# The early rows of the first expert get tiles of their own and are loaded inside the attention pipeline

## The chip, the core and the metric

One core of a Trainium2 chip runs the kernel. The metric is the device time of one execution in microseconds (us), the median of three runs. The engines have a program each and meet through semaphores: TensorE (PE, matmuls and transposes), VectorE (DVE), ScalarE (ACT), GpSimd (POOL), and SyncE (SP), which only issues transfers (DMA). An engine takes its instructions strictly in the order of its program.

## The reference

Chunked local attention is followed by a mixture of experts. The shapes are 4 batches, 8 heads, 768 positions, 64 per head; queries go in chunks of 32 that see 16 positions to the left, 8 to the right and 8 memory positions.

```python
scores = scale * np.matmul(q_c, k_full.transpose(0, 1, 3, 2))
scores = scores - np.max(scores, axis=-1, keepdims=True)
a = np.exp(scores)
a = a / (np.sum(a, axis=-1, keepdims=True) + 1e-09)
out[:, :, c_start:c_end] = np.matmul(a, v_full)
```

The result is read as 3072 tokens of 512 numbers. Each token goes to the one of 8 experts whose logit is largest, at most 768 tokens to an expert, first come first served, and the result is weighted with the softmax probability.

```python
logits = x @ w_gate
expert_idx = np.argmax(logits, axis=1)
...
h = np.maximum(np.einsum('ecd,edf->ecf', disp, w1), 0.0)
y = np.einsum('ecf,efd->ecd', h, w2)
```

All is fp32. Each expert matmul is done as three: both operands are split into a high part and the remainder (`hi` and `lo`), and hi·hi, lo·hi and hi·lo are added.

## The kernel before, in words

**Attention** runs over 24 tiles of 128 tokens, steps t = 0 to 23. In one step PE does the scores of tile t (L508), transposes of keys or queries for later tiles (trans_k L474, trans_q L462), the transposes of the exponentials of tile t-1 (`trans_p`, L532), the product with the values of tile t-2 (`value`, L549), the transposes of the attention output of tile t-3 (`trans_out`, L602), and, once per group of tiles, the routing logits (L626, for the last group L617). DVE takes the row maximum m (L516) and the difference d (L519), scales the output (rc L552 and L554, xr L557) and copies overlapping value rows into the next value tile vw (L413, L414). SP loads values and weights in program order. What is left after step 23 is called the drain: trans_p(23), value(22), value(23) and what follows them.

**Routing** is done for seven groups of tiles, (first tile, number): (0,4), (4,4), (8,4), (12,4), (16,3), (19,3), (22,2), numbered 0 to 6. `route(g)` is a chain of short DVE rows with PE work in between: r_m, r_d, r_t, r_idx, r_oh (the one-hot choice, L660), then PE counts the tokens ahead (L665 to L669), then r_sel, r_cnt, `seen` (the running count per expert, L680), r_den, r_pos, r_ov, r_slot, r_dst. It is a Python generator, and `tick` lets it go on by one row, so the places of the ticks set where these rows stand in each engine's program. When r_dst is there, POOL puts the group's token rows into the DRAM buffer x_d by indirect transfers, one per tile (`put`, L796): each row goes to its slot with its expert. After the last group the finish chain (L709 to L741) works out the counts, the slots to be filled with padding (`pads`) and flags for the branches.

**Early rows** are the first 256 rows (two tiles) of expert 0. They are complete once group 3 has been routed if at least 256 tokens have chosen expert 0 by then; the flag `ok` says so. `early_rows` loads them into xg (L309) after the last value product; `early` transposes them (L322), multiplies them with w1 of expert 0 (layer 1, L331 and L340) and applies relu (L341, L342), in pieces that the ticks of groups 5 and 6 are interleaved with. Each of the eight pieces f holds 12 matmuls. w2 is split into w2hi and w2lo (`split2`, ACT L847 and DVE L848). Their layer 2 (L911) stands at the start of `expert(0)`.

**Experts.** For each expert: load its rows (`load_x`, L818), transpose them (`trans_x`, L832, with xhi on ACT L836 and xlo on DVE L837), layer 1 (L856), relu (L869, L870), layer 2 (L911), scaling (y, L917) and an indirect store of the tokens (L918). For expert 0 the transposes stand between pieces of the second half of the early layer 2. `values` loads flags into registers of the engines. `fill(e)` writes padding rows to the unused slots of expert e (POOL).

## Time and profile before

| what | value |
|---|---|
| median of 3 runs (lowest, highest) | 512.57 us (512.25, 512.99) |
| profiled execution, its own time | 512.2 us |
| span of its instructions | 510.3 us |
| mean granted PE clock | 0.974 of full |
| busy: PE, DVE, ACT, POOL | 464.8, 303.3, 240.0, 117.0 us |
| start of scores(20), (21), (22), (23) | 119.13, 124.63, 130.36, 135.57 us |
| early rows: load issued, first transpose | 149.56, 153.55 us |
| early layer 2, first and expert 0's layer 1, first | 170.48, 183.61 us |

The page gives each engine's busy time, the waits and the chain of work that ended last; timelines list single rows with their start, duration and the idle time ahead of them with what ended it. Idle time of PE can be read in brackets; the granted clock is read from rows by windows of time. DMA rows show when a transfer was issued and the chain how long it took to land.

### The profile page before, as it was taken

Reading aid. Unit: us, or ns where it says so; the run is one execution under the profiler, and the core shown is the slowest. Engines: PE = TensorE matmul, PEld = TensorE weight load, DVE = VectorE, ACT = ScalarE, POOL = GpSimd, SP = SyncE. Lnnn points to the kernel's source line nnn. Section 1 sums busy time; section 2 is a strip of 40 time slices with the busy share of each in tenths; the row PEclk is TensorE's granted clock in tenths of the full one; section 3 lists DMA queues with packets and bytes.
Section 4 is the critical chain, followed back from the end, with each engine's and each line's share of the span. In section 5 each row is a group of like instructions: output and inputs, shape, how many; then the busy total and the mean of one; then the engine's idle time right before and its main releaser. Section 6 shows DMA issues by size and latency. Waiting matters only on the chain.

```text
span 510.3 us, 11844 instructions
## 1 busy us (share of the span) xinstructions
PE 464.8 (91%) x4321; PEld 397.0 (78%) x4321; DVE 303.3 (59%) x673; ACT 240.0 (47%) x462; POOL 117.0 (23%) x151
## 2 busy tenths in 40 slices
PE   7789997998859898998999999999999799699993
PEld 6677876776649788886778899799888788687882
DVE  5989797999945742565644535655434365655410
ACT  6698787788622432534444234434412353453300
POOL 7531134554624370110200200100021002010011
PEclk9999999999987998999999999999999799999998
DMA  9687879974672484355363281461413343640010
GB/s 208 141 211 178 201 238 268 214 194 109 150 261 96 163 316 143 134 185 181 123 226 116 100 296 33 170 207 56 166 62 111 134 166 104 211 182 9 3 41 38
DMA packets 77775, 78.44 MB, mean 154 GB/s; under 512 B 31762, under 2 KB 58510, under 8 KB 77648
## 3 DMA queue, kind: packets, MB, share of 16 engines
q1 hardware_dynamic: 72848, 61.93, 41.8%
q0 software_dynamic: 4800, 14.95, 7.6%
q8 instruction: 64, 1.05, 0.8%
q14 instruction: 63, 0.52, 0.3%
HBM read 60.86 MB, written 15.99 MB: 151 GB/s over the span
## 4 chain that ended last, share of the span: by engine, by line
DMA 39%; issue 32%; PE 13%; DVE 7%; ACT 2%; POOL 2%; SPq 2%; POOLq 1%; DVEq 0%; ACTq 0%
DMA out_dram<-y,tok 30%; DMA x_d<-pad,pads 4%; PE ps L549 3%; PE ps L508 2%; PE ps L462 2%; DMA x_d<-xr,r_dst 2%; ACT kw L479 2%; DVE vw L414 1%; PE ps L602 1%; PE ps L331 1%; PE ps L474 1%; DMA vw<-in_v_dram 1%; DMA memv<-in_mem_v_dram 1%; PE ps L532 1%; POOL vw L135 1%
## 5 line engine op out<-in xcount | busy, mean ns | idle before, releaser
L869 ACT ACTIVATE hhi<-p 128x512 fp32r<-128x512 f32 x68 | 40.7, 598 | 146.5 <-PE p L856 116.7
L918 POOL DMA_INDIRECT out_dram<-y,tok x28 | 31.8, 1134 | 282.7 <-DVEq L840 148.8
L870 DVE SCALAR_TENSOR_TENSOR hlo<-p,hhi 128x512 fp32r<-128x512 f32 x68 | 47.0, 691 | 77.2 <-ACT hhi L869 72.8
L911 PE MATMUL p<-w2hi,hhi 128*128 128x512 f32 x224 | 91.6, 409 | 1.3 <-DVE hlo L342 1.3
L911 PE MATMUL p<-w2lo,hhi 128*128 128x512 f32 x224 | 88.0, 393 | 0.0
L911 PE MATMUL p<-w2hi,hlo 128*128 128x512 f32 x224 | 87.6, 391 | 0.0
L856 PE MATMUL p<-xhi,w1hi 128*128 128x320 f32 (+3 forms) x288 | 61.0, 334 | 9.4 <-DVEq L900 5.6
L856 PE MATMUL p<-xhi,w1lo 128*128 128x320 f32 (+3 forms) x288 | 59.1, 328 | 0.0
L856 PE MATMUL p<-xlo,w1hi 128*128 128x320 f32 (+3 forms) x288 | 58.7, 326 | 0.0
L856 PEld LDWEIGHTS p<-xhi,w1hi 128*128 128x128 f32 x288 | 47.0, 195 | 13.1 <-issue 5.2
L917 DVE TENSOR_SCALAR y<-p,xg 128x512 f32<-128x512 f32 x28 | 21.0, 749 | 53.7 <-PE p L911 32.2
L911 PEld LDWEIGHTS p<-w2hi,hlo 128*128 128x128 f32 x224 | 42.1, 188 | 9.9
L856 PEld LDWEIGHTS p<-xhi,w1lo 128*128 128x128 f32 x288 | 47.4, 194 | 2.8
L911 PEld LDWEIGHTS p<-w2hi,hhi 128*128 128x128 f32 x224 | 42.2, 188 | 9.4 <-ACT w2hi L847 1.4
L856 PEld LDWEIGHTS p<-xlo,w1hi 128*128 128x128 f32 x288 | 47.0, 192 | 2.8
L911 PEld LDWEIGHTS p<-w2lo,hhi 128*128 128x128 f32 x224 | 42.2, 188 | 7.6
L837 DVE TENSOR_TENSOR xlo<-px,xhi 128x512 fp32r<-128x512 f32 x34 | 23.3, 690 | 32.0 <-ACT xhi L836 32.0
L479 ACT COPY kw<-ps 64x256 f32<-64x256 f32 x92 | 35.5, 386 | 11.8 <-PE ps L474 10.5
L848 DVE TENSOR_TENSOR w2lo<-raw,w2hi 128x512 fp32r<-128x512 f32 x64 | 41.0, 682 | 0.0
L836 ACT CAST xhi<-px 128x512 fp32r<-128x512 f32 x34 | 19.8, 588 | 43.8 <-PE px L832 36.3
L822 DVE TENSOR_TENSOR w1lo<-raw,w1hi 128x512 fp32r<-128x512 f32 x56 | 36.6, 685 | 2.9 <-ACT w1hi L821 1.0
L847 ACT CAST w2hi<-raw 128x512 fp32r<-128x512 f32 x64 | 36.1, 618 | 0.0
(154 smaller groups left out, 707.8 us busy)
## 6 DMA issues: line engine op xcount, KB each, us to landing
raw<-in_moe_w_dram SPq DMA_DIRECT2D x16, 2048.0 KB
raw<-in_q_dram SPq DMA_DIRECT2D x11, 512.0 KB
raw<-in_k_dram SPq DMA_DIRECT2D x10, 512.0 KB
vw<-in_v_dram SPq DMA_DIRECT2D x57, 64.0 KB
xg<-x_d SPq DMA_DIRECT2D x3, 792.0 KB
vw<-in_v_dram SPq DMA_DIRECT2D x31, 72.0 KB
xg<-x_d SPq DMA_DIRECT2D x4, 528.0 KB
xg<-x_d SPq DMA_DIRECT2D x2, 1056.0 KB
```

What stands on the lines that cost most here:

```text
L479: (nc.vector.tensor_copy if n == 0 and i else nc.scalar.copy)(out=kw[r, 2 * i:2 * i + 2, :, hf, 24 + j:56:2], in_=ps[j * 64:j * 64 + 64, h ...
L822: (eng or self.nc.vector).tensor_tensor(out=lo[sl], in0=raw[sl], in1=hi[sl].bitcast(F32), op=ALU.subtract)
L836: nc.scalar.copy(out=self.xhi[:, d:d + k, sl], in_=pv)
L837: nc.vector.tensor_tensor(out=self.xlo[:, d:d + k, sl], in0=pv, in1=self.xhi[:, d:d + k, sl].bitcast(F32), op=ALU.subtract)
L847: self.nc.scalar.copy(out=self.w2a[:, j], in_=self.raw2[:, j])
L848: self.nc.vector.tensor_tensor(out=self.w2b[j // 4][:, j % 4], in0=self.raw2[:, j], in1=self.w2a[:, j].bitcast(F32), op=ALU.subtract)
L856: self.nc.tensor.matmul(ps, a[:, d, fs], b[:, d, o:o + w], start=(i + d == 0), stop=(i == 2 and d == KD - 1))
L869: self.nc.scalar.activation(out=self.hhi[hs], in_=ps, func=AF.Relu)
L870: self.nc.vector.scalar_tensor_tensor(out=self.hlo[hs], in0=ps, scalar=0.0, in1=self.hhi[hs].bitcast(F32), op0=ALU.max, op1=ALU.subtract)
L911: self.nc.tensor.matmul(ps, a[:, f, t * P:t * P + P], b, start=(f == 0 and i == 0), stop=(f == KF - 1 and i == 2))
L917: nc.vector.tensor_scalar(out=y, in0=ps, scalar1=self.xg[e % 2][:, t, D:D + 1], scalar2=None, op0=ALU.mult)
L918: nc.gpsimd.indirect_dma_start(out=self.out[:, :], out_offset=bass.IndirectOffsetOnAxis(ap=tok[:, t:t + 1], axis=0), in_=y, in_offset=None ...
```

## The change

The early rows get tiles of their own (`xga`, `xhia`, `xloa`, and `hhia`, `hloa` for the hidden rows), which exist from the start or from the drain on, so that their load needs no tile of the expert stage. The first 256 rows of x_d are filled with padding at t = 4, so that the load can be made without asking `ok` first. `ok` itself is computed at the end of the chain of group 3 instead of group 4. The routing of group 3 is ticked on in step 20 (three ticks) and finished in step 21, ahead of trans_q, and all puts up to group 3 follow there. The load is issued in step 22, after load_v and ahead of the load of w2. The eight transposes of the early rows stand at the end of step 23, ahead of trans_p(23) and value(22). The eight layer-1 pieces run in the drain and in the routing of the last groups, one after every sixth tick, and the rest with the first splits of w2. `load_x(0)` is issued first in `experts`, then the rest of w2 is split, and the early layer 2 runs in one piece ahead of the memset of four banks, of two of the three register loads, of the fills of experts 1 to 7 and of the transposes of expert 0's rows.

```diff
@@ attention
+            if t == 4:
+                nc.sync.dma_start(out=self.x_d[0:EARLY, :].rearrange("(t p) w -> p t w", p=P),
+                                  in_=self.pad[:, None, :].broadcast_to([P, TA, XW]))
...
             self.scores(t)
+            if t == 21:
+                while min(self.done) <= GA:
+                    self.tick(True)
+                while self.puts and self.puts[0][2] <= GA:
+                    self.put(*self.puts.pop(0)[:2])
...
             self.exps(t)
+            if t == 20:
+                for _ in range(3):
+                    self.tick(True)
...
-            if t == 22:
+            if t == NTL - 2:
+                self.early_rows()
+            if t == NTL - 2:
 
                 nc.sync.dma_start(out=self.raw2, in_=self.w2[0].rearrange("(k p) d -> p k d", p=P))
...
+            if t == NTL - 1:
+                phase = self.early()
+                run(KD)
...
         self.value(L)
-        self.early_rows()
         self.logits(L - 3)
...
         self.trans_out(L - 1)
         self.tick(True)
+        run(1)
         self.logits(L - 2)
...
         for _ in range(4):
             self.tick(True)
+        run(1)
         self.logits(L - 1)
         self.logits(L)
         self.routes.append([self.route(ends[L]), 1])
-        run(KD)
-        wait = 3
+        n = 0
         while self.routes:
             self.tick(True)
-            run(int(wait <= 0))
-            wait -= 1
+            n += 1
+            run(int(n % 6 == 0))
...
-        self.finish_routing()
-        run(4)
         self.todo2 = list(range(KF))
-        for _ in range(3):
+        for _ in range(4):
             self.split2(self.todo2)
-            run(3)
+            run(1)
@@ early
-        for g, ge in ((0, 3), (3, 6), (6, 8)):
...
+        for f in range(KF):
+            ps = self.psum()[:, 0:EARLY]
+            self.mm1(ps, f, True, EARLY)
+            self.relu(ps, True, f, slice(0, EARLY))
+            yield
@@ route
-        if g == GA + 1:
...
         nc.vector.tensor_tensor(out=self.seen, in0=self.seen, in1=cnt, op=ALU.add)
+        if g == GA:
+            yield 1
+            po = self.lgp[0:1, 3 * P + 32 * ((g + 1) % 4) + 24:3 * P + 32 * ((g + 1) % 4) + 32]
+            nc.tensor.matmul(po, self.ones[:, 0:1], self.seen, start=True, stop=True)
+            nc.vector.tensor_scalar(out=self.ok, in0=po[:, 0:1], scalar1=float(EARLY), scalar2=None, op0=ALU.is_ge)
+            self.okd = True
@@ experts
+        self.yes = self.values(self.ok, ENGS, 2)[0]
+        with tc.If(self.yes > 0):
+            tok = self.tokens(0, 0, TA)
+            for t in range(TA):
+                self.layer2(0, t, tok)
+        for ps in self.p1:
+            nc.vector.memset(ps[:, WIDTHS[0]:], 0.0)
...
@@ expert
         if not e:
-
-            with tc.If(self.yes > 0):
-                tok = self.tokens(e, 0, TA)
-                for t in range(TA - 1):
-                    self.layer2(e, t, tok)
-            ps = self.p2[self.order.index(TA - 1)]
-            for i, fs in enumerate((range(0, 3), range(3, 6), range(6, KF))):
-                with tc.If(self.yes > 0):
-                    self.mm2(ps, TA - 1, fs)
-                    if fs[-1] == KF - 1:
-                        self.put_y(e, ps, TA - 1, tok)
-                self.trans_x(e, i, 1)
-            self.trans_x(e, KD - 1, 1)
+            for d in range(KD):
+                self.trans_x(e, d, 1)
```

The change moves instructions in three places that matter below. The first is PE in steps 20 and 21; before, the counts of group 3 (L665 to L669) stood behind value(19):

```order
L508 MATMUL ps<-kw_102,qT 32x128 x16
L462 MATMUL ps<-ident,raw_69 64x128 x16
L532 MATMUL ps<-ident,d 128x128 x4
L549 MATMUL ps<-vw_105,pT 32x130 x16
L665 LDWEIGHTS ones
L665 MATMUL lgp<-seen,ones 128x32
```

and now the last of them stand ahead of scores(21), with the new one-column matmul for `ok` (L675) ahead of trans_q (L457):

```order
L662 MATMUL lgp<-r_oh,ones 128x8
L664 LDWEIGHTS upper
L664 MATMUL lgp<-r_oh,upper 128x32
L503 MATMUL ps<-kw_105,qT 32x128 x16
L675 LDWEIGHTS ones
L675 MATMUL lgp<-seen,ones 1x8
L457 MATMUL ps<-ident,raw_69 64x128 x16
```

The line numbers of the changed kernel differ by a few: L503 is its scores, L527 its trans_p, L544 its value product, L597 its trans_out. The second place is PE at the end of step 23, where the transposes of the early rows (L331, tile xga) now stand ahead of trans_p(23) and value(22):

```order
L544 MATMUL ps<-vw_107,pT 32x130 x16
L636 MATMUL ps<-ident,lT 128x96
L597 MATMUL ps<-ident,xr 128x128 x4
L331 MATMUL ps<-ident,xga 128x128 x8
L527 MATMUL ps<-ident,d 128x128 x4
L544 MATMUL ps<-vw_108,pT 32x130 x16
L597 MATMUL ps<-ident,xr 128x128 x4
```

Before, eight transposes (L322) of the same kind stood behind the last logits. The third place is PE from the end of the early layer 2 to the layer 1 of expert 0 (L863); the sixteen transposes of expert 0's rows (L838) and two register loads now stand behind the last layer-2 matmul (L921):

```order
L921 MATMUL p_0_3072<-w2lo_3081,hhia 128x512
L921 MATMUL p_0_3072<-w2hi,hloa 128x512
L776 UNCONDITIONAL_BRANCH x2
L793 TENSOR_LOAD m_80
L793 TENSOR_LOAD big
L838 MATMUL px<-ident,xg_2755 128x128 x16
L846 COMPARE_AND_BRANCH
```

Before, the transposes (there L832) were spread over the second half of that layer 2 in pieces of four.

More of the change, by code (lines that the diff above doesn't have):

```diff
@@ L184, in attention, with run @@
         todo = list(range(0, F, SPLIT1))
+        phase = iter(())
+        def run(n):
+            for _ in range(n):
+                next(phase, None)
         def split1(t):
@@ L242, in attention @@
         L = NTL - 1
-        phase = self.early()
-        def run(n):
-            for _ in range(n):
-                next(phase, None)
         self.trans_p(L)
@@ L253, in attention @@
         self.value(L)
-        self.early_rows()
         self.logits(L - 3)
         self.tick(True)
+        self.c_st.close()
+        self.mw, self.c_mw = self.pool("mw", bufs=1, reuse_waits="tile")
+        assert self.nt <= TA + TB
+        self.hhia = self.mw.tile([P, KF, EARLY], F32R, name="hhia")
+        self.hloa = self.mw.tile([P, KF, EARLY], F32R, name="hloa")
+        self.xg = [self.mw.tile([P, TB, XW], F32, name="xg0")]
+        self.xhi = self.mw.tile([P, KD, TB * P], F32R, name="xhi")
+        self.xlo = self.mw.tile([P, KD, TB * P], F32R, name="xlo")
+        self.hhi = self.mw.tile([P, KF, TB * P], F32R, name="hhi")
+        self.hlo = self.mw.tile([P, KF, TB * P], F32R, name="hlo")
+        nc.gpsimd.memset(self.xg[0][:, :, 0:D + 2], 0.0)
         self.trans_out(L - 1)
         self.tick(True)
+        run(1)
         self.logits(L - 2)
@@ L314, in early @@
     def early(self):
         nc, te = self.nc, EARLY // P
-        xg, xhi, xlo = self.xg[0], self.xhi, self.xlo
-        ps = [None] * KD
         for d in range(KD):
-            ps[d] = self.psum()[:, 0:EARLY]
+            ps = self.psum()[:, 0:EARLY]
             for t in range(te):
-                nc.tensor.transpose(out=ps[d][:, t * P:(t + 1) * P], in_=xg[:, t, d * P:(d + 1) * P], identity=self.ident)
-            nc.scalar.copy(out=xhi[:, d, 0:EARLY], in_=ps[d])
+                nc.tensor.transpose(out=ps[:, t * P:(t + 1) * P], in_=self.xga[:, t, d * P:(d + 1) * P], identity=self.ident)
@@ L324, in early @@
+            nc.scalar.copy(out=self.xhia[:, d, :], in_=ps)
+            nc.vector.tensor_tensor(out=self.xloa[:, d, :], in0=ps, in1=self.xhia[:, d, :].bitcast(F32), op=ALU.subtract)
             yield
[L325 to L344 removed]
@@ L669, in route @@
         nc.tensor.matmul(pp[:, 0:w * E], self.upper, oh, start=False, stop=True)
-        if g == GA + 1:
-            nc.tensor.matmul(pp[0:1, 24:32], self.ones[:, 0:1], self.seen, start=True, stop=True)
-            nc.vector.tensor_scalar(out=self.ok, in0=pp[0:1, 24:25], scalar1=float(EARLY), scalar2=None, op0=ALU.is_ge)
-            self.okd = True
         sel = sm.tile([P, w, E], F32, name="r_sel", bufs=3)
@@ L774, in experts @@
         nc.sync.dma_start(out=self.raw1, in_=self.w1[1].rearrange("(k p) f -> p k f", p=P))
-        for e in range(1, E):
-            self.fill(e)
-        nc.gpsimd.memset(self.xg[1][:, :, 0:D + 2], 0.0)
+        while self.todo2:
+            self.split2(self.todo2)
         full = self.values(self.full, ET.Pool, 2)[0]
@@ L811, in load_x @@
             if a == 1:
-                nc.sync.dma_start(out=xg[:, 0:TA, :], in_=self.x_d[o:o + EARLY, :].rearrange("(t p) w -> p t w", p=P))
+                nc.sync.dma_start(out=self.xg1a if e % 2 else self.xga, in_=self.x_d[o:o + EARLY, :].rearrange("(t p) w -> p t w", p=P))
             if a:
@@ L849, in split2, with mm1 @@
                                      op=ALU.subtract)
-    def mm1(self, ps, f, o, w):
+    def mm1(self, ps, f, first, w):
         fs = slice(f * P, (f + 1) * P)
-        for i, (a, b) in enumerate(((self.w1hi, self.xhi), (self.w1lo, self.xhi), (self.w1hi, self.xlo))):
+        hi, lo = (self.xhia, self.xloa) if first else (self.xhi, self.xlo)
+        for i, (a, b) in enumerate(((self.w1hi, hi), (self.w1lo, hi), (self.w1hi, lo))):
             for d in range(KD):
-                self.nc.tensor.matmul(ps, a[:, d, fs], b[:, d, o:o + w], start=(i + d == 0), stop=(i == 2 and d == KD - 1))
+                self.nc.tensor.matmul(ps, a[:, d, fs], b[:, d, 0:w], start=(i + d == 0), stop=(i == 2 and d == KD - 1))
     def bank(self):
@@ L892, in layer1 @@
             for ps, f in zip(pss, fs):
[L893 removed]
+                self.relu(ps, False, f, slice(0, TB * P))
             for _ in fs:
```

105 lines of the change are left out of this document (40 added, 65 removed).

## The prediction

> **What bounds the kernel now.** I read the page's busy shares first, then the timeline of TensorE (PE) through the end of the attention pipeline, then the chain that ended last for the same stretch. Rows of the timelines are: start us, duration, engine, line, operation, out<-in, tile shapes, count, and in brackets the idle time of the engine before the row with what ended it.
>
> ```profile
> span 510.3 us, 11844 instructions
> ...
> PE 464.8 (91%) x4321; PEld 397.0 (78%) x4321; DVE 303.3 (59%) x673; ACT 240.0 (47%) x462; POOL 117.0 (23%) x151
> ```
>
> PE is busy 91% of the span, so over the whole kernel PE is the bound, and the expert stages after 184 us are not touched in their matmuls. The change acts between step 20 (119 us) and the first layer 1 of expert 0 (183.61 us), and there the question is where PE stands still.
>
> ```profile
> 140.14 1.10 PE L549 MATMUL ps<-vw,pT 128*32 128x130 f32 x32
> ...
> 145.49 1.89 PE L617 MATMUL ps<-wg,xT 128*128 128x32 f32 x16
> 153.55 1.94 PE L322 MATMUL ps<-ident,xg 128*128 128x128 f32 x8 [6.17 <-DMA xg<-x_d]
> ...
> 170.48 0.47 PE L911 MATMUL p<-w2hi,hhi 128*128 128x512 f32 x1 [1.28 <-DVE hlo L342]
> ...
> 182.51 1.03 PE L832 MATMUL px<-ident,xg 128*128 128x128 f32 x8
> ...
> 183.61 1.08 PE L856 MATMUL p<-xhi,w1hi 128*128 128x320 f32 x4
> ```
>
> The large hole is 6.17 us: PE has done the attention (last logits 145.49 + 1.89 = 147.38) and waits for the early rows. Their layer 1 follows, and layer 2 from 170.48 to 182.51: 48 matmuls and eight transposes of expert 0's rows among them (the last eight, at 182.51, take 1.03), so a layer-2 matmul takes (12.0 - 1.0) / 48 = 0.23. Behind a hole the clock falls:
>
> ```profile
> 85.50:87.75 2.25, 0.01 (x1) 0.03 (x1) 1.44 (x3) 2.16 (x6) 0.59 (x1) 1.00 0.70 187
> 87.75:89.00 1.25, 1.25 (x28) 1.25 (x32) 1.25 (x4) 0.07 (x1) 0.63 (x2) 0.57 1.14 333
> 157.00:158.50 1.50, 1.50 (x11) 1.41 (x10) 0.88 (x9) 0.00 (x0) 0.70 (x1) 0.50 0.65 253
> 191.50:193.50 2.00, 0.02 (x2) 0.00 (x0) 0.69 (x1) 0.60 (x1) 0.00 (x0) 1.00 0.04 13
> 193.50:195.00 1.50, 1.42 (x6) 1.43 (x7) 0.00 (x0) 0.00 (x0) 0.00 (x0) 0.58 0.59 132
> 195.00:197.00 2.00, 2.00 (x9) 2.00 (x9) 0.00 (x0) 0.00 (x0) 0.00 (x0) 0.50 0.49 183
> ```
>
> In these rows by windows the three last numbers are the granted clock, the DMA share and GB/s. After 6.17 us of idleness the clock is still 0.50 at 158.5 us, some 5 us of work at half speed. A hole of about 2 us (191.50 to 193.50) was enough as well: 0.58 and 0.50 until 197.00, which is some 3.2 us at half speed or 1.6 us lost. A removed hole is therefore worth more than its width, and a new one costs more.
>
> The chain (start, duration, what) says why the rows are late, the view of the row buffer x_d how long its transfers take, and two issue rows what stands ahead; the chain's last row here is one piece of 12 layer-1 matmuls at full clock, 1.43:
>
> ```profile
> 140.27 9.04 DMA x_d<-xr,r_dst
> 149.56 3.86 DMA xg<-x_d
> ...
> 160.55 1.43 PE ps L340 x12
> ...
> DMA to landing us min/median/max: 2.8/5.2/9.3
> ...
> 136.37 0.99 POOL L796 DMA_INDIRECT x_d<-xr,r_dst  x1 [2.48 <-DVE r_dst L701]
> ...
> 130.93 5.44 SPq L390 DMA_DIRECT2D vw<-in_v_dram  x8
> ```
>
> The last put of routing group 3 leaves at 140.27 and takes 9.04 us, among the slowest of its kind (median 5.2), and the load takes 3.86 us.
>
> **Term 1: routing moved into steps 20 and 21.** VectorE (DVE) is the busy engine there. It makes each routing row and each softmax row, and PE stands in program order behind them.
>
> ```profile
> 124.63 1.08 PE L508 MATMUL ps<-kw,qT 128*32 128x128 f32 x32
> ...
> 129.70 0.22 PE L667 MATMUL lgp<-r_oh,ones 128*128 128x24 bf16 x3 [0.33 <-DVE r_oh L660]
> ...
> 132.57 0.38 PE L549 MATMUL ps<-vw,pT 128*32 128x130 f32 x2 [0.54 <-issue]
> ...
> 124.61 0.51 DVE L495 COPY kw<-kw 64x672 f32<-64x672 f32 x1 [0.35 <-ACT kw L479]
> ...
> 127.03 0.17 DVE L644 TENSOR_REDUCE r_m<-ps 128x4 f32<-128x32 f32 x1
> 127.13 0.67 DVE L516 TENSOR_REDUCE m<-ps 128x8 f32<-128x512 f32 x1
> ...
> 127.94 0.68 DVE L519 TENSOR_TENSOR d<-ps,m 128x512 f32<-128x512 f32 x1
> ...
> 129.39 0.26 DVE L660 TENSOR_TENSOR r_oh<-r_t,r_idx 128x32 bf16<-128x32 f32 x1
> ...
> 129.79 0.76 DVE L557 TENSOR_TENSOR xr<-ps,rc 128x256 f32<-128x256 f32 x2
> 130.56 0.28 DVE L413 COPY vw<-vw 24x256 f32<-24x256 f32 x1
> ```
>
> Now the routing chain r_m to r_oh stands right behind the kw copy, which ends at 125.12. Seven short rows at about 0.17 us make r_oh ready near 126.2. PE would have been free for scores(21) at 124.63 and is held by the matmuls that read r_oh: 1.6 us. Scores then take 1.08 us, and the next matmul in PE's order reads `seen`, which DVE makes only after the reciprocal, the xr pair (0.76), a vw copy (about as long as m), m (0.67) and d (0.68) of tile 21: about 129.6, while PE is through scores at 127.5. That is a second wait of 2.0 us, with nothing behind it that could go first, because trans_q(11), trans_p and value all stand behind that matmul. One value of it is `ok`, which no PE work needs. DVE starves in turn for some 1.5 us. The first copy into the next vw tile (130.56) comes near 134.2: **+3.6**. Bounds: +0.7, if only the first wait stays and takes the place of the 0.33 and 0.54 us that PE stands idle today in the same steps (1.6 - 0.9); +4.6, if the second wait also halves the clock for 2 us, as the 2-us hole at 191.5 did.
>
> **Term 2: where value(22) starts.** The load of the early rows is issued by SP behind the eight value loads (130.93, 5.44 us long, gated by those vw copies), so SP reaches it near 140.2 rather than at once. The puts of group 3 now follow one another: r_dst is ready near 130.8, and with two puts of group 2 ahead and 1.3 us each (four from 136.37 to 140.27), the last leaves near 135.7. With the median 5.2 us it lands near 141, and 3.86 us later, near 145, the rows are there. PE, 3.6 us late, has done its step-23 work near 142.4 and finds the eight transposes of the early rows ahead of trans_p(23) and value(22): a wait of 2.6 us in place of 6.17, but in front of attention work instead of behind it. The transposes (1.0 us at full clock, 1.94 in the row at half), say 1.5, and trans_p, 0.5, put value(22) at 147.0 against 140.14: **+6.9**. Bounds: +1.6, if term 1 is at its low end and the rows are in time (0.7, plus 0.9 of transposes); +11.0, if the last put takes 9.3 us. I take the median because the puts no longer share their time with the 5.44 us of value loads, as far as the order shows. The prefill at t=4 is one more transfer on SP far ahead of all this; I take it at nothing, covered by PE's work there, and at most the 2.8 us of the fastest put if the loads behind it wait it out.
>
> **Term 3: value(22) to the end of the finish chain.**
>
> ```profile
> 163.44 0.17 DVE L711 COPY f_n<-lgp 128x8 f32<-128x8 f32 x1 [0.26 <-PE lgp L709]
> ...
> 166.73 0.14 DVE L741 TENSOR_SCALAR full<-f_top 1x1 int32<-1x1 f32 x1
> 166.80 0.40 DVE L342 SCALAR_TENSOR_TENSOR hlo<-ps,hhi 128x256 fp32r<-128x256 f32 x1
> 167.13 0.67 DVE L848 TENSOR_TENSOR w2lo<-raw,w2hi 128x512 fp32r<-128x512 f32 x1
> ```
>
> Before, from 140.14 to 166.87: 26.7 us, and groups 5 and 6 stood behind the hole in PE's order. Now: 5.35 from value(22) to the last logits (145.49 - 140.14), two layer-1 pieces (2 x 1.43 = 2.86), those logits (1.89), the chain of group 6, 4.1 (about two dozen short rows of 0.17, partly in pairs, with PE's answers between), four hlo rows among them (4 x 0.42 = 1.7), and the finish chain from the PE row ahead of 163.44 to 166.87 (3.6). Sum 19.5: **-7.2**. This is the gain, the 6.17-us hole and some of the slow clock. I see no reason that it should vanish; 2 us either way.
>
> **Term 4: finish chain to layer 2 of the early rows.** Layer 2 needs the low halves of w2 and of the hidden rows from DVE. Before, from 166.87 to 170.48: 3.6. Now four w2lo and four hlo stand behind the finish chain, 4 x (0.67 + 0.40) = 4.3, less 0.06 where each w2lo row overlaps the next, 4.05: **+0.45**. PE has four pieces for 3.6 + 4.05 us, 5.7 us of work, and stands idle for about 2 us before layer 2, in place of the 1.28 of the row above, which kept the clock.
>
> **Term 5: layer 2 to the first layer 1 of expert 0.**
>
> ```profile
> 173.52 1.09 DVE L768 MEMSET p<- 128x256 f32 x4
> 175.44 0.17 DVE L924 CAST tok<-xg 128x2 int32<-128x2 f32 x1 [0.82 <-DMA xg<-x_d]
> 176.27 0.75 DVE L917 TENSOR_SCALAR y<-p,xg 128x512 f32<-128x512 f32 x1 [0.66 <-PE p L911]
> ...
> 178.78 0.59 ACT L836 CAST xhi<-px 128x512 fp32r<-128x512 f32 x1 [6.57 <-PE px L832]
> ...
> 179.40 0.69 DVE L837 TENSOR_TENSOR xlo<-px,xhi 128x512 fp32r<-128x512 f32 x1 [2.38 <-ACT xhi L836]
> ```
>
> Before, 13.1 us (170.48 to 183.61): 48 matmuls x 0.23 = 11.0, half the transposes of expert 0's rows between them (1.0), the other half and a branch behind (1.1). ACT and DVE split the transposed rows while PE multiplied. Now layer 2 runs in one piece, 11.0, and behind it nothing covers the rest: DVE makes the last y (0.75), the memset of four banks (1.09) that stood under layer 2 before, two register loads (up to 0.8 by the 0.82 idle above, where three were), then the first xlo (0.69), which frees a bank for the third and fourth transposes (two xlo 1.4, four transposes 0.35, xhi 0.59): 5.0. Adding the slow clock behind the idle time of term 4, 1.6 as at 193.5: 17.6, **+4.5**. Bounds: +1.4 if the register loads and memset are hidden and the clock stays (11.0 + 3.5); +6.2 if the tail's own hole halves the clock again.
>
> All later stages shift as a whole: the fills, behind the early scatters on POOL now, are still some us ahead of the loads that need them.
>
> **Sum.** 6.9 - 7.2 + 0.45 + 4.5 = +4.65. The profiled execution took 512.2 (span 510.3 and 1.9 around it), so 516.9; it stands 0.4 below the median of the runs, 512.57, so I write **517.0**.
>
> The Trainium skill, page "TensorE: Matmul & The Clock Gate", section "Part 1: The HAM clock gate", lets the clock fall only after an idle window of about 3.4 us, free-running. The 2.25 us before 87.75 and the 2.0 us before 193.50 disagree: both lowered it. By the rule alone no new hole here would lower it, and the sum would be an estimated 514.3, the rival B below.
>
> **Rivals.** About 0.2%, 1 us, is what a measurement of this kernel can tell from no change.
> A, faster: the routing fits into the idle slots of steps 20 and 21, the rows are in time, and the tail of term 5 is at its low end: 1.6 - 7.2 + 0.45 + 1.4 = -3.75, **508.4**. For it: SP, POOL and ACT have room, and the gain of term 3 is by far the surest. Against it: DVE shows hardly any idle time from 124.61 to 130.56, and the order puts PE behind `seen`. It decides if PE waits less than 1 us in step 21.
> B, the clock stays: holes of 2.6 and 2 us without the half clock, as the 1.28-us one before 170.48; 1.6 less in term 5 and 1.0 less in term 2, **514.3**. Against it stand the windows quoted.
> C, no change: rows in time (value(22) about +2.5), the tail as forecast: 2.5 - 7.2 + 0.45 + 4.5 = +0.25, **512.4**.
> D, slower still: the last put takes 9.3 us as before, the early rows land near 149, and attention itself waits for them: 516.9 + 4.1 = **521.0**. For it: both DMA rows of the chain. It decides once the put takes over 6 us.
>
> **Chances.** Forecast 0.47, A 0.19, B 0.11, C 0.11, D 0.12. The forecast's own range is 514.5 to 519.5; the range to hold 8 in 10 is 509.0 to 521.5, cutting off part of A and D. Faster 0.19, same 0.11, slower 0.70.
>
> **What would show it.** In the changed profile: a PE wait of some 2 us at the one-column `ok` matmul (L675) ahead of trans_q; a PE wait on the xga load before its transposes, and value(22) near 147; the finish chain's end some 20 us after value(22); PE idle for about 2 us before layer 2 with a granted clock near 0.5 behind; and some 5 us between the last layer-2 matmul and expert 0's layer 1. If DVE has `seen` ready early, or the tail is under 3 us, the forecast falls towards A.

## The result

The changed kernel takes 517.95 us (median of 14 runs, 513.28 to 520.51) against 511.41 us (14 runs, 506.20 to 513.53): a ratio of 1.013, 95% interval 1.0092 to 1.0167. It is slower, by about the forecast amount. On another chip, later, the same two kernels gave 528.9 and 516.06 us, 1.0262 (1.022 to 1.0305), so the loss is not the same everywhere. The kernel before, run as if it were a variant, gave 1.0026 (0.9986 to 1.0065), so differences under some 0.4% are not told apart below. "First chip" is a name here for the place of the two first profiles; which chip that was is not on record.

The profiled execution of the changed kernel, the longest of its 14, took 520.51 us with a span of 518.7, 8.4 more than the profile before. These are the rows of its timeline on TensorE (PE) that answer to those of before; line numbers are the changed kernel's (L457 trans_q, L527 trans_p, L544 value, L331 the early rows' transposes, L921 layer 2, L863 layer 1):

```profile
128.83 0.22 PE L662 MATMUL lgp<-r_oh,ones 128*128 128x24 bf16 x3 [1.76 <-DVE r_oh L655]
...
132.04 0.17 PE L675 MATMUL lgp<-seen,ones 128*1 128x8 bf16 x1 [1.95 <-DVE seen L671]
132.14 3.68 PE L457 MATMUL ps<-ident,raw 128*64 128x128 f32 x32
135.75 1.12 PE L527 MATMUL ps<-ident,d 128*128 128x128 f32 x4
136.80 1.65 PE L544 MATMUL ps<-vw,pT 128*32 128x130 f32 x32
...
151.13 1.46 PE L331 MATMUL ps<-ident,xga 128*128 128x128 f32 x8 [3.00 <-DMA xga<-x_d]
...
153.38 1.89 PE L544 MATMUL ps<-vw,pT 128*32 128x130 f32 x32
...
178.03 0.47 PE L921 MATMUL p<-w2hi,hhia 128*128 128x512 f32 x1 [2.66 <-DVE hloa L879]
...
195.46 1.12 PE L863 MATMUL p<-xhi,w1hi 128*128 128x320 f32 x4 [0.17 <-ACT xhi L842]
...
205.68 0.45 PE L863 MATMUL p<-xhi,w1hi 128*128 128x320 f32 x2 [0.87 <-issue]
```

All four waits of the forecast are there: 1.76 us for r_oh, 1.95 us for `seen`, 3.00 us for the early rows, 2.66 us ahead of layer 2. At three of them the clock fell, as the rows by windows show (granted clock, DMA share and GB/s last). At the second it fell while PE still stood idle, between 131.10 and 131.20; and it was low once more from 165.40 to 168.70, behind no hole over 0.7 us:

```profile
130.50:131.10 0.60, 0.00 (x0) 0.00 (x0) 0.60 (x2) 0.20 (x1) 0.60 (x1) 1.00 0.00 0
131.20:132.00 0.80, 0.00 (x0) 0.00 (x0) 0.79 (x3) 0.00 (x0) 0.64 (x2) 0.50 0.00 0
132.10:134.00 1.90, 1.90 (x19) 1.86 (x20) 1.10 (x8) 0.00 (x0) 1.59 (x2) 0.50 0.36 142
134.00:136.00 2.00, 2.00 (x19) 1.67 (x16) 0.00 (x0) 0.75 (x2) 1.39 (x3) 0.50 0.43 167
...
153.00:155.00 2.00, 2.00 (x35) 1.44 (x33) 0.72 (x4) 0.71 (x3) 0.00 (x0) 0.50 0.73 281
...
165.40:168.70 3.30, 3.30 (x18) 3.30 (x17) 0.66 (x5) 0.38 (x1) 0.00 (x0) 0.50 0.19 75
...
180.00:182.00 2.00, 2.00 (x6) 1.60 (x5) 1.01 (x2) 0.00 (x0) 0.00 (x0) 0.50 0.07 13
```

On VectorE (DVE) the rows that set the milestones, and in the chain of waits the load of the early rows:

```profile
131.84 0.16 DVE L671 TENSOR_TENSOR seen<-seen,r_cnt 128x8 bf16<-128x8 bf16 x1
...
139.73 0.99 DVE L408 COPY vw<-vw 24x256 f32<-24x256 f32 x1
...
173.97 0.14 DVE L738 TENSOR_SCALAR full<-f_top 1x1 int32<-1x1 f32 x1
...
190.95 0.75 DVE L927 TENSOR_SCALAR y<-p,xga 128x512 f32<-128x512 f32 x1 [4.78 <-PE p L921]
191.90 1.09 DVE L781 MEMSET p<- 128x256 f32 x4 [0.20 <-PE px L838]
193.29 1.29 DVE L843 TENSOR_TENSOR xlo<-px,xhi 128x512 fp32r<-128x512 f32 x2 [0.30 <-issue]
```

```profile
145.57 5.43 DMA xga<-x_d
```

The first vw copy stands at 139.73 instead of 130.56, value(22) at 153.38 instead of 140.14, the end of the finish chain at 174.11 instead of 166.87, and behind the last layer-2 matmul come y, memset and xlo in a row with PE uncovered.

One trace is one execution. What follows rests on a table of milestones, read from the timelines of all kernels (start in us of the scores of step 20 to 23, of value(22), of the last finish row, of the early layer 2 and of layer 1 of experts 0 and 1; then the span). The last column is the ratio to the kernel before on the same chip. The rows "another chip", "no prefill" and "ok, rows, tail" come from chip 2, the rows from "ok late" to "tail as before" from chip 3 and the last four from chip 6. On chips 3 and 6 the kernel before ran beside the variants, but not the changed kernel itself.

| kernel | 20 | 21 | 22 | 23 | value(22) | finish | layer 2 | exp. 0 | exp. 1 | span | ratio |
|---|---|---|---|---|---|---|---|---|---|---|---|
| before, first chip | 119.0 | 124.6 | 130.4 | 135.4 | 140.1 | 166.7 | 170.5 | 183.6 | 220.9 | 510.3 | 1 |
| before, another chip | 119.1 | 124.8 | 130.8 | 136.5 | 143.7 | 167.6 | 175.2 | 191.4 | 226.1 | 514.0 | 1.003 |
| changed, first chip | 121.5 | 129.0 | 139.0 | 144.6 | 153.4 | 174.0 | 178.0 | 195.5 | 231.1 | 518.7 | 1.013 |
| changed, another chip | 122.1 | 129.6 | 141.1 | 146.5 | 155.2 | 175.9 | 181.9 | 200.3 | 238.8 | 528.9 | 1.026 |
| ok late | 120.6 | 128.2 | 133.3 | 146.8 | 152.0 | 171.7 | 178.3 | 195.5 | 232.5 | 522.1 | 1.015 |
| PE kept busy | 120.8 | 128.3 | 139.9 | 145.8 | 153.1 | 173.0 | 179.9 | 198.1 | 235.0 | 521.8 | 1.016 |
| rows late | 119.9 | 127.5 | 139.1 | 144.5 | 148.8 | 168.5 | 175.8 | 193.5 | 230.0 | 517.9 | 1.015 |
| tail as before | 121.2 | 128.7 | 140.4 | 145.8 | 154.7 | 174.5 | 181.8 | 196.8 | 237.0 | 523.2 | 1.016 |
| no prefill | 118.6 | 126.2 | 137.4 | 143.1 | 151.5 | 172.3 | 179.0 | 197.2 | 234.0 | 521.2 | 1.018 |
| ok, rows, tail | 119.5 | 127.1 | 132.2 | 145.7 | 150.4 | 171.3 | 177.7 | 192.2 | 233.7 | 522.1 | 1.018 |
| the same, fills too | 121.7 | 129.3 | 137.9 | 147.3 | 151.7 | 173.1 | 178.8 | 196.2 | 231.4 | 520.4 | 1.004 |
| and routing moved | 120.3 | 126.0 | 132.1 | 140.2 | 145.1 | 168.0 | 174.3 | 190.7 | 224.5 | 512.2 | 1.000 |
| and puts in two lots | 121.4 | 127.1 | 133.1 | 139.5 | 145.4 | 170.4 | 176.8 | 193.4 | 227.9 | 514.8 | 1.003 |
| ok late, puts later | 121.1 | 128.6 | 133.7 | 139.7 | 147.8 | 170.7 | 176.9 | 195.1 | 232.1 | 520.3 | 1.013 |

### The profile page after: what moved, and what is told of

Read it like the earlier page. It is cut to its first block, busy times and chain, and to the rows that moved or that the text cites. A ratio compares the mean times of both kernels' runs of the same rounds, so it can differ in the third digit from the quotient of the medians.

```text
span 518.7 us, 11812 instructions
## 1 busy us (share of the span) xinstructions
PE 469.9 (91%) x4321; PEld 401.1 (77%) x4321; DVE 303.6 (59%) x681; ACT 240.4 (46%) x462; POOL 115.7 (22%) x152
## 4 chain that ended last, share of the span: by engine, by line
PE 38%; issue 22%; DMA 21%; DVE 8%; POOL 3%; SPq 3%; ACT 2%; POOLq 1%; DVEq 0%; ACTq 0%
DMA out_dram<-y,tok 16%; PE p L921 13%; PE p L863 12%; PE ps L544 3%; DMA x_d<-xr,r_dst 3%; PE ps L457 3%; PE ps L503 2%; ACT kw L474 2%; DMA raw<-in_mem_v_dram 1%; DVE vw L409 1%; PE ps L597 1%; PE ps L527 1%; PE px L838 1%; SPq L391 1%; DMA xga<-x_d 1%
## 5 line engine op out<-in xcount | busy, mean ns | idle before, releaser
L921 PE MATMUL p<-w2hi,hhi 128*128 128x512 f32 x192 | 78.7, 410 | 0.0
L921 PE MATMUL p<-w2lo,hhi 128*128 128x512 f32 x192 | 75.5, 393 | 0.0
L921 PE MATMUL p<-w2hi,hlo 128*128 128x512 f32 x192 | 75.2, 392 | 0.0
L863 PE MATMUL p<-xhi,w1hi 128*128 128x320 f32 (+3 forms) x256 | 55.4, 339 | 7.8 <-DVEq L909 2.8
L863 PE MATMUL p<-xlo,w1hi 128*128 128x320 f32 (+3 forms) x256 | 53.7, 333 | 0.0
L863 PE MATMUL p<-xhi,w1lo 128*128 128x320 f32 (+3 forms) x256 | 53.6, 332 | 0.0
L863 PEld LDWEIGHTS p<-xhi,w1hi 128*128 128x128 f32 x256 | 42.2, 194 | 11.5 <-issue 5.8
L863 PEld LDWEIGHTS p<-xlo,w1hi 128*128 128x128 f32 x256 | 42.7, 193 | 2.8
L863 PEld LDWEIGHTS p<-xhi,w1lo 128*128 128x128 f32 x256 | 42.6, 193 | 2.8
L921 PEld LDWEIGHTS p<-w2hi,hlo 128*128 128x128 f32 x192 | 36.1, 188 | 8.4
L474 ACT COPY kw<-ps 64x256 f32<-64x256 f32 x92 | 35.6, 387 | 13.0 <-PE ps L469 11.8
L921 PEld LDWEIGHTS p<-w2hi,hhi 128*128 128x128 f32 x192 | 36.2, 189 | 6.7
L921 PEld LDWEIGHTS p<-w2lo,hhi 128*128 128x128 f32 x192 | 36.2, 189 | 6.4
L544 PE MATMUL ps<-vw,pT 128*32 128x130 f32 x768 | 30.6, 293 | 8.9 <-issue 4.8
```

The costliest lines, as they stand in the source:

```text
L474: (nc.vector.tensor_copy if n == 0 and i else nc.scalar.copy)(out=kw[r, 2 * i:2 * i + 2, :, hf, 24 + j:56:2], in_=ps[j * 64:j * 64 + 64, h ...
L544: nc.tensor.matmul(ps[32 * c4:32 * c4 + 32, i * 130:i * 130 + 130], pT[:, pr * P + 32 * c4:pr * P + 32 * c4 + 32], vw[:, c + c4 + 1, :, pr ...
L863: self.nc.tensor.matmul(ps, a[:, d, fs], b[:, d, 0:w], start=(i + d == 0), stop=(i == 2 and d == KD - 1))
L921: self.nc.tensor.matmul(ps, a[:, f, o:o + P], b, start=(f == 0 and i == 0), stop=(f == KF - 1 and i == 2))
```

## The experiments

**One part undone at a time.** The theory was the forecast's: three places (steps 20 and 21, the place of the early rows, the tail), whose prices add up. Four variants of the changed kernel ran on one chip. The first puts the flag `ok` back into the routing of group 4:

```diff
@@ route
+        if g == GA + 1:
+            nc.tensor.matmul(pp[0:1, 24:32], self.ones[:, 0:1], self.seen, start=True, stop=True)
+            nc.vector.tensor_scalar(out=self.ok, in0=pp[0:1, 24:25], scalar1=float(EARLY), scalar2=None, op0=ALU.is_ge)
...
-        if g == GA:
-            yield 1
-            po = self.lgp[0:1, ...]
-            nc.tensor.matmul(po, self.ones[:, 0:1], self.seen, start=True, stop=True)
...
```

> The changed kernel with the flag ok computed in the routing of group 4, as before the change, so that TensorE (PE) no longer stands behind `seen` in step 21. Theory 1 (the loss is made in steps 20 and 21): the second wait (1.95 us in the changed kernel's trace) goes, the granted clock stays at 1.0 behind it, and trans_q, trans_p and value (3.68, 1.12, 1.65 us) take 1.97, 0.66, 1.10 again: 4 to 5 us less than the changed kernel, so about 1.004 of the kernel before. Rival (the loss is made by the transfers of the early rows, which do not move with PE): the wait of 3.0 us on xga grows by what step 21 gains, under 1 us less than the changed kernel, about 1.012. Rival (the loss is made in the tail before expert 0's layer 1): same, 1.012.

The second gives PE 9 and 10 transposes of the identity to do in the two waits, into a bank that nothing reads:

```diff
@@ route
+        if g == GA:
+            self.busy(9)
         pp = self.lgp[:, ...]
...
         if g == GA:
             yield 1
+            self.busy(10)
             po = self.lgp[0:1, ...]
```

> The changed kernel with 9 and 10 idle transposes of the identity (about 0.15 us each) on PE ahead of the two waits of steps 20 and 21, so that PE is not idle there. Theory (the slow clock behind the second wait is a cost of its own, 2.7 us): the waits stay, filled, and trans_q, trans_p and value run at full clock: 2 to 3 us less than the changed kernel, about 1.008. Rival (only the waits count, DVE is late anyway): within 1 us of the changed kernel, 1.013, or up to 0.5 us above it.

The third moves the early rows' transposes behind value(23):

```diff
-            if t == NTL - 1:
-                phase = self.early()
-                run(KD)
...
         self.value(L)
+        phase = self.early()
+        run(KD)
         self.logits(L - 3)
```

> The changed kernel with the eight transposes of the early rows behind value(23), so that no attention work stands behind their load. Theory 2 (the early rows come too late for their place in front of trans_p(23)): the wait of 3.0 us and the slow clock behind it (about 2 us) go, trans_p(23) and both value products fill them: 3 to 5 us less than the changed kernel, about 1.005. Rival (the chain of the last groups is bound by the routing rows on DVE, not by PE): the time moves into waits on DVE later in the drain, under 1.5 us less, 1.011.

The fourth puts memset, register loads and the transposes of expert 0's rows back to where they were:

```diff
+        for ps in self.p1:
+            nc.vector.memset(ps[:, WIDTHS[0]:], 0.0)
         self.yes = self.values(self.ok, ENGS, 2)[0]
...
+        for i, fs in enumerate((range(0, 3), range(3, 6), range(6, KF))):
+            with tc.If(self.yes > 0):
+                self.mm2(ps, TA - 1, fs)
...
+            self.trans_x(0, i, 1)
```

> The changed kernel with the end of the early layer 2 as before: memset and all three register loads ahead of layer 2, and the transposes of expert 0's rows between pieces of its second half. Theory 3 (the uncovered tail costs 4.3 us, 17.4 against 13.1 from the first layer-2 matmul to expert 0's layer 1): that distance is 13 to 14.5 us again, and the whole 3 to 4.5 us less than the changed kernel, about 1.005. Rival (the later stage gives it back: in the changed trace the PE hole in the middle of expert 0's layer 1 is 0.87 us with full clock, before it was 2.06 with a slow clock behind): the hole returns, 1 to 1.5 us less than the changed kernel, about 1.010.

Measured: 1.015 (1.0106 to 1.0194), 1.0156 (1.0116 to 1.0197), 1.0149 (1.0106 to 1.0193) and 1.0162 (1.0113 to 1.0211). The expectations were about 1.004, 1.008, 1.005 and 1.005, so all four fell. How much each variant gained against the changed kernel can't be said from the ratios, because that kernel did not run on their chip, and it gave 1.013 in one place and 1.026 in another. The traces say more of where a gain went. With `ok` late, the second wait is gone and scores(22) come 5.1 us after scores(21) instead of 10.0, but scores(23) come 13.5 us after that. From scores(20) to scores(23) this variant takes 26.2 us, the one with PE kept busy 25.0, and the changed kernel 23.1 and 24.5 in its two profiles: by then nothing of the gain is left. These are PE, ScalarE (ACT), DVE and GpSimd (POOL) in the variant with `ok` late, in this order:

```profile
133.32 0.86 PE L503 MATMUL ps<-kw,qT 128*32 128x128 f32 x7
134.51 0.43 PE L503 MATMUL ps<-kw,qT 128*32 128x128 f32 x6 [0.33 <-issue]
...
139.58 0.66 PE L503 MATMUL ps<-kw,qT 128*32 128x128 f32 x5 [0.36 <-issue]
```

```profile
139.63 0.59 ACT L599 COPY xT<-ps 128x512 f32<-128x512 f32 x1 [6.25 <-remote]
```

```profile
139.57 0.16 DVE L547 TENSOR_SCALAR rc<-ps 128x4 f32<-128x4 f32 x1 [4.84 <-remote]
```

```profile
130.93 1.01 POOL L797 DMA_INDIRECT x_d<-xr,r_dst  x1 [0.16 <-issue]
...
137.41 0.99 POOL L797 DMA_INDIRECT x_d<-xr,r_dst  x1 [0.30 <-issue]
```

PE, which has nothing to wait for by the program, gets through its scores in pieces of a few matmuls; ACT and DVE stand still until 139.6, but for one row of DVE at 134.56, with inputs that PE finished at 133.4. From 130.93 to 138.4 POOL issues six puts one behind the other, two of group 2 and the four of group 3. Keeping PE busy tells the same: the clock stays at 1.00, trans_q is back at 1.97 us, and the step still ends at 139.8.

```profile
131.48 1.97 PE L462 MATMUL ps<-ident,raw 128*64 128x128 f32 x32
...
136.81 0.40 PE L549 MATMUL ps<-vw,pT 128*32 128x130 f32 x3 [0.45 <-issue]
...
139.79 0.35 DVE L552 TENSOR_SCALAR rc<-ps 128x4 f32<-128x4 f32 x2 [6.95 <-remote]
```

So in these traces nothing came of removing the wait or the slow clock alone: the step ended between 139 and 140 us all the same. With the rows late, value(22) comes sooner than in the two profiles of the changed kernel (148.8 against 153.4 and 155.2), and the finish chain too (168.5 against 174.0 and 175.9), but layer 2 starts at 175.8 against 178.0 and 181.9. With the tail as before, layer 2 to expert 0 takes 15.0 us instead of 17.4 and 18.4, but expert 0 itself 40.2 instead of 35.6 and 38.5.

**Controls, the sum of three, and the prefill.** On another chip ran the two kernels themselves, the changed kernel with the three parts undone at once, and the changed kernel without the prefill of x_d at t = 4 (the lines that the change adds there).

> The kernel before the change, once more, for a trace from the same chip as the runs beside it. No theory is at stake: ratio 1.00.

> The changed kernel, once more, beside the others. All theories: 1.013. If ScalarE (ACT) stands still for several us among the last early relu rows here too, as in four variants whose undone part gained nothing (waits that the profile puts down to a remote releaser, beside packets of the instruction queues), then code loading is a cost of the changed kernel on this chip; if not, it belongs to the variants.

> The changed kernel with three parts undone at once: the flag ok in group 4's routing, the transposes of the early rows behind value(23), the tail as before. Theory (three terms that add up: steps 20 and 21, the place of the early rows, the tail): 0.998 to 1.004. Rival (ACT waits for its code among the last early relu rows, whatever PE gained ahead of it, so early layer 2 starts at the same time in all of them): within 2 us of the changed kernel, 1.010 or more.

> The changed kernel without the prefill of the first 256 rows of x_d at t = 4 (left out: the padding for the case of fewer than 256 early tokens, which these inputs do not have). Theory: the prefill is off the path, within 1 us of the changed kernel, 1.013. Rival (it delays the value loads on SP, and the hole of PE at step 15, 3.75 us in the changed trace and 2.25 before, is its price): about 1.5 us less, 1.010.

Measured: 1.0026 (0.9986 to 1.0065), 1.0262 (1.022 to 1.0305), 1.0179 (1.013 to 1.0229) and 1.0184 (1.0135 to 1.0234). Here the changed kernel ran beside its variants. Three parts undone gain 0.8%, far from the 2.6% of the theory, which falls: the prices do not add up. Its rival, that all starts of layer 2 are alike because ACT stands still there, is half right: ACT does stand still among the last early relu rows (waits of 2.1 to 5.7 us that the profile puts down to a remote releaser) in eleven of the fourteen traces, but in that of the kernel before on this chip as well, so it is no cost of the change alone. It stands beside a row of indirect transfers: in that trace POOL issues five puts and a fill back to back from 163.58 to 170.94, and ACT goes on at 172.13. In the two first profiles the same row of transfers goes with no such wait. The views of ACT's waits, first of the kernel before on this chip, then of the variant with the rows late (seconds named: total, times, longest, in us):

```profile
ACT hhi L342 <- remote: 3.9, 1, 3.9
```

```profile
ACT hhia L877 <- remote: 5.7, 1, 5.7
```

The prefill surprised: without it the ratio is 0.8% lower than with it on the same chip (medians 528.9 and 523.4 us; the two intervals overlap a little), and scores(20) start at 118.6 against 122.1. The theory of at most 1 us falls, and the gain is more than the rival's 1.5 us. The hole of PE at step 15, ahead of a value product, is 1.97 us without the prefill and 3.75 with it:

```profile
90.89 1.10 PE L544 MATMUL ps<-vw,pT 128*32 128x130 f32 x32 [3.75 <-issue]
```

```profile
87.38 1.10 PE L541 MATMUL ps<-vw,pT 128*32 128x130 f32 x32 [1.97 <-issue]
```

Over the table, scores(20) start at 118.6 to 119.1 in the three traces without a prefill and at 119.5 to 122.1 in the eleven with it, 2.0 us later on the mean. That is one trace each, and the hole varies among kernels with the prefill too, so the price is some 2 us and its path through the transfers is not shown.

**Are the puts the second limit?** In the variant with `ok` late, the four puts of group 3 were moved behind value(23):

```diff
             if t == 21:
                 while min(self.done) <= GA:
                     self.tick(True)
-                while self.puts and self.puts[0][2] <= GA:
+                later = [p for p in self.puts if p[2] == GA]
+                self.puts = [p for p in self.puts if p[2] < GA]
+                while self.puts:
                     self.put(*self.puts.pop(0)[:2])
...
         self.value(L)
+        for p in later:
+            self.put(*p[:2])
```

> The variant with the flag ok in group 4's routing, and the four puts of group 3 issued behind value(23), behind the load of the early rows (left out by that: the early rows of tiles 12 to 15, which are padding then). Theory (six puts back to back on POOL hold up the other engines: in the variant with ok late, scores(22) comes 5.1 us after scores(21), but scores(23) 13.5 us after that, with ACT and DVE idle until 139.6, when the puts' packets end): scores(22) to scores(23) is 5 to 6.5 us. Rival (the standstill is the load of code, or of the value rows, and the puts only stand beside it): 10 us or more, as with the puts.

Scores(22) to scores(23) took 6.0 us (133.7 to 139.7) in place of 13.5. And a standstill appeared where the puts had gone, with four puts in a row. POOL, PE and ACT of that kernel:

```profile
131.35 1.01 POOL L801 DMA_INDIRECT x_d<-xr,r_dst  x1 [0.16 <-issue]
132.66 0.98 POOL L801 DMA_INDIRECT x_d<-xr,r_dst  x1 [0.30 <-issue]
...
147.01 1.01 POOL L801 DMA_INDIRECT x_d<-xr,r_dst  x1 [9.68 <-DMA xga<-x_d]
...
150.88 0.98 POOL L801 DMA_INDIRECT x_d<-xr,r_dst  x1 [0.30 <-issue]
```

```profile
150.82 0.19 PE L666 MATMUL lgp<-r_oh,ones 128*128 128x16 bf16 x2 [1.29 <-issue]
...
152.66 0.83 PE L548 MATMUL ps<-vw,pT 128*32 128x130 f32 x18 [0.98 <-issue]
```

```profile
152.80 0.59 ACT L603 COPY xT<-ps 128x512 f32<-128x512 f32 x1 [4.11 <-remote]
```

The rival, that code or value rows were late and the puts only stood beside it, falls: the steps run freely where the puts are not. That code arrives late because of the puts is not ruled out by this. In the six later traces with a standstill of ACT or DVE at these puts it ends 0.8 to 1.3 us after POOL has issued the last of them. The whole is 1.0128 (1.0074 to 1.0183), so moving the standstill is no gain.

**The fills, the routing, the lots.** Three more variants build on the one with three parts undone. The first issues the seven fills, and two memsets of POOL that follow them, ahead of the early layer 2, as before the change; the second also moves the block of step 21 behind that step's value product and drops the ticks of step 20; the third splits its six puts into three in step 21 and the rest in step 22.

```diff
@@ experts
+        for e in range(1, E):
+            self.fill(e)
         while self.todo2:
@@ attention, the second
-            if t == 20:
-                for _ in range(3):
-                    self.tick(True)
...
                 self.value(t - 2)
+            if t == 21:
+                while min(self.done) <= GA:
+                    self.tick(True)
+                while self.puts and self.puts[0][2] <= GA:
+                    self.put(*self.puts.pop(0)[:2])
@@ attention, the third
-                while self.puts and self.puts[0][2] <= GA:
+                for _ in range(3):
                     self.put(*self.puts.pop(0)[:2])
+            if t == 22:
+                while self.puts and self.puts[0][2] <= GA:
+                    self.put(*self.puts.pop(0)[:2])
```

> The variant with three parts undone, and the fills of experts 1 to 7 issued ahead of the early layer 2 as before the change. Theory (the seven fills back to back on POOL are what holds ACT up at the branch in expert 0's layer 1, where PE has a hole of 5.3 us in that variant and 5.5 in the one with the tail alone): the hole is under 2.5 us, and the whole about 1.010. Rival (the hole is code loading at the taken branch and has nothing to do with the fills): 4 us or more, 1.018.

> The one before, with the routing of group 3 finished behind the step's value product in step 21 and no ticks in step 20, so that PE waits for no routing row ahead of scores(21) or trans_q. Theory (what is left of term 1): scores(21) to scores(22) about 6 us, no wait over 1 us on r_oh, 3 us less than the variant beside it; with all four terms undone and the early rows loaded early, 0.995 to 1.003. Rival (the six puts in a row hold the engines up wherever they stand): scores(22) to value(22) stays 17 us or more, 1.010.

> The one before, with three puts in step 21 and the rest in step 22 in place of six in a row. Theory (the burst is the cost): 2 to 5 us less than that one, 0.988 to 0.998. Rival (the number of puts in a row does not matter): the same within 1 us.

Measured: 1.0037 (1.0004 to 1.007), 1.0005 (0.9974 to 1.0036) and 1.0032 (0.9994 to 1.007). By the ratios the fills were the largest step, 1.0179 to 1.0037, but those are from two chips, and the two spans differ by 1.7 us only, so the step is read from the traces. In the variant with three parts undone the fills, behind the early scatters, ran under the branch in expert 0's layer 1, where ACT stood still for 6.48 us and PE for 5.32:

```profile
193.60 0.97 POOL L804 DMA_INDIRECT x_d<-pad,pads  x1 [0.30 <-issue]
...
201.27 0.97 POOL L804 DMA_INDIRECT x_d<-pad,pads  x1 [0.30 <-issue]
```

```profile
203.69 1.08 ACT L883 ACTIVATE hhi<-p 128x512 fp32r<-128x512 f32 x2 [6.48 <-remote]
```

```profile
205.07 1.43 PE L868 MATMUL p<-xhi,w1hi 128*128 128x320 f32 x4 [5.32 <-DVE hlo L884]
```

With the fills ahead, they end at 194 and the hole is 1.63 us, under the 2.5 of the theory:

```profile
185.33 0.97 POOL L804 DMA_INDIRECT x_d<-pad,pads  x1 [8.21 <-DMA xg<-x_d]
...
193.01 0.98 POOL L804 DMA_INDIRECT x_d<-pad,pads  x1 [0.30 <-issue]
```

```profile
205.13 0.84 PE L868 MATMUL p<-xhi,w1hi 128*128 128x320 f32 x4 [1.63 <-DVEq L914]
```

From layer 2 to expert 1 this is 52.7 us against 56.0; the tail itself is longer with the fills in it (17.5 us from layer 2 to expert 0, against 14.5). Over all traces PE's hole at this branch is 0.87 to 5.53 us in the nine with the fills under it and at most 2.06 in the five with the fills ahead, so the fills go with a larger hole, but not everywhere with a large one: the 0.87 is the changed kernel's in its first profile. With the routing moved as well, scores(21) to scores(22) are 6.0 us, scores(22) to value(22) 13.0 in place of the rival's 17, and the kernel is level with the one before (its interval lies below both of the changed kernel's): value(22) to the finish chain takes 22.9 us (145.1 to 168.0) instead of 23.9 to 26.6 in the two profiles of before, but value(22) itself comes 1.4 to 5.0 us later, so that by these traces the early load gains about what it costs. Two lots instead of one, expected to gain 2 to 5 us, make no difference that can be told (1.0032 against 1.0005), though ACT and DVE show no standstill in steps 22 and 23 there and scores(22) to (23) take 6.4 us instead of 8.1: the rows then land later, and PE waits 2.70 us for them. No variant beats the kernel before.

## Why the prediction was right, point by point

The sign, the size (517.0 forecast) and the range held on the first chip (the 528.9 of the other lies outside), but not by the working throughout. All four waits came where they were forecast; the sizes of two terms and the shift of the later stages were wrong, and these errors have opposite signs, so that the sum came near by luck. By the milestones of the two first profiles:

- **Term 1** had both waits right (1.76 and 1.95 us, forecast 1.6 and 2.0) and was too small. The first vw copy comes 9.2 us later, 2.5 of which PE had lost by step 20 (121.46 against 118.95), so 6.7 against a forecast of 3.6 and an upper bound of 4.6. What it left out of the likeliest case, and sized at 1.0 in the bound, was the half clock at the second wait: trans_q 3.68 instead of 1.97, trans_p 1.12 instead of 0.66, value 1.65 instead of 1.12, together 2.7. And it counted the six puts in a row as time of POOL alone; in later traces, where the wait or the slow clock was gone, other engines stood still beside them.
- **Term 2**: value(22) moves by 13.2, 10.7 without the loss ahead of step 20; forecast 6.9. The difference is the 3.1 that term 1 was short of, and that the load left at 145.57, when SP came to it behind the value loads, and not when the last put landed (its packets had ended by 141.8), and took 5.43 us instead of 3.86. PE's wait was 3.0 (forecast 2.6). Rival D's shift of value(22), 11.0, was nearly reached, by another mechanism than D's late put.
- **Term 3**: 20.7 us from value(22) to the end of the finish chain, forecast 19.5, so -6.0 against before, where -7.2 was forecast. The working had full clock here. The half clock from 165.40 to 168.70 lies on two layer-1 pieces ahead of the finish chain's matmul: from 164.96 to 169.41 they take 4.45 us in place of 2.86.
- **Term 4**: 3.9 us (4.05), with 2.66 us of idle PE (2) and the clock at 0.50 behind it.
- **Term 5**: 17.4 us (17.6), the closest, and by its own parts: 12.7 us of layer 2, first at half clock (11.0 and 1.6), and 4.7 behind it (5.0). But the variants show that its price is not all its own: with the tail alone undone the hole at expert 0's branch is 5.53 us, where the changed kernel has 0.87 and 3.98, and takes the gain back.
- **The prefill**, taken at nothing with a bound of 2.8, costs about 2 us by the traces up to step 20, and some 4 by the ratios; that is argued from 14 traces and one timed variant, not settled.
- **Later stages**, taken as a mere shift, gave 3.4 us back in this pair of profiles (11.9 us late at expert 0, 8.4 at the end), so "all later stages shift as a whole" was wrong. Of that, 1.7 lie in expert 0 (35.6 us against 37.3): the hole of 2.06 us at 193.58 is 0.87 at 205.68. A stretch of half clock is in both, behind that hole before, and now behind the tail's own hole of 2.25 us, ahead of 194.03. Another 1.6 lie in the layer 1 that starts at 399.60 (389.11 before), where PE's hole is 2.82 us instead of 3.57; why is open. On the other chip the same place had a hole of 3.98, and expert 0 took 38.5 us against 34.7 before, 3.8 of the 14.9 us between the spans there.

2.5 + 10.7 - 6.0 + 0.3 + 4.3 = 11.8 and -3.4 make the 8.4 of the two spans within rounding; the forecast's 4.65 is nearer to the 6.5 of the medians than it deserves. In the traces the loss is 2.5 us ahead of step 20, 6.7 in steps 20 and 21, 4.0 from there to value(22), with the early transposes, and 4.3 in the tail; the closed hole gives 6.0 back.

Rival B, that the clock stays, fell: at three of the four new waits the clock went to 0.50. The rule of the Trainium skill (page "TensorE: Matmul & The Clock Gate", "Part 1: The HAM clock gate"), by which only an idle window of about 3.4 us lowers it, does not hold here: no hole at these waits is that long. But the forecast's own rule, that a hole of 2 us lowers it, does not hold either. The clock of the changed kernel fell 1.1 us into the hole of 1.95 us, which a hole of 1.76 us stood close ahead of, and a hole of 1.75 us alone was enough in the variant with the fills moved (0.50 from 129.50 to 132.90). A hole of 2.25 us left it at 1.00 in the kernel before on the other chip (88.45), and so did 3.20 us in the variant with the rows late:

```profile
89.38 1.10 PE L543 MATMUL ps<-vw,pT 128*32 128x130 f32 x32 [3.20 <-issue]
```

```profile
89.40:92.50 3.10, 3.10 (x78) 2.53 (x80) 3.06 (x13) 1.53 (x3) 0.00 (x0) 1.00 0.93 189
```

In the traces the clock changes at intervals of 3.41 us or a multiple (0.50 from 193.73 to 197.14 before the change, from 131.18 to 138.00 behind it). Counted back in such steps from its later changes, a step of the variant with the rows late begins at 87.64, within that hole, and divides it into 1.5 and 1.7 us. So it may be the idle time within one step that decides; nothing here tested that, and the price of a hole is uncertain by the 1.7 us that one step at half clock loses.

The Trainium skill says on the page "Runtime: NRT & Kernel Launch", section "Instruction fetch mechanics", that a taken branch can force a load of code before the engine goes on; at expert 0's branch ACT stands still as that would have it, but moving the fills and their two memsets took PE's hole from 5.32 to 1.63 us, so the branch by itself is not the 5 us.

## What to carry to other kernels

When undoing a cost gains nothing, look for a second limit that ends at the same time: here the step ended between 139 and 140 us whether PE had waited, run slowly or run freely before, just behind the last of six puts (issued by 139.1, 138.5 and 138.4 us). An indirect transfer that looked free because its engine was idle went with standstills of other engines when several followed one another, so a step that gathers them, or moves them next to work that has no slack, is worth a run of its own. An early start of one transfer is worth only what stands behind it in program order: here the eight transposes for rows that were not there yet took back 4.0 of the 6.0 us that the closed hole gave. And a variant is to be run beside the changed kernel itself on the same chip: four ratios without it could not say what each part cost.

## What the runs showed of the hardware

- Six indirect puts in a row (7.5 us of POOL) go with a standstill of ACT (up to 6.25 us) or DVE (up to 6.95 us) and a PE that issues a few matmuls at a time, without any wait in the program. It moves when the puts move (4.11 us on ACT at the new place), and the like is seen at the fills (6.48 us on ACT). What the engines lack in that time is open: in the variant with `ok` late the view of the DMA queues shows one packet of an instruction queue in 133 to 134 us and none from there to 150, and the releaser is given only as remote.
- Such standstills are not in every execution: in the two first profiles no wait of ACT or DVE behind 100 us is put down to a remote releaser, and in each of the twelve later traces the longest is 2.1 to 7.0 us. The kernel before shows it on the other chip: 3.9 us on ACT, and a value(21) that PE issues in three pieces beside its four puts; its span is 3.7 us longer there. Whether the chip makes the difference is not shown.
- The length of a PE hole alone does not tell whether the clock falls: it fell at holes of 1.75, 1.95 (with one of 1.76 close ahead), 2.66 and 3.00 us, and stayed at 1.00 at holes of 2.25, 2.70 (in the variant with the puts in two lots, 150.95) and 3.20. Once down it stayed at 0.50 for 3.41 us or a multiple. With 19 idle transposes placed in the two holes of steps 20 and 21 it stayed at 1.00 there.
